# Attention and two expert layers on one core: the instruction order laid out by another scheduling model

## The chip, the cores and the metric

The kernel runs on one core of a Trainium2 chip. The metric is the device time of one launch in microseconds (us); lower is better. A core has several engines that run side by side, each with its own list of instructions that it works through in order: PE (TensorE: matrix products, with PEld for its weight loads), DVE (VectorE) and ACT (ScalarE) for elementwise work, POOL (GpSimd) for elementwise work as well, and SP (SyncE), which here issues nearly all transfers (DMAs). An instruction that needs the result of another engine waits at the head of its list, and everything behind it on that engine waits with it.

## The reference

Three layers follow each other. For 4 batches and 8 heads of 576 positions with 64 features, the attention is the sum of two parts; then come two layers on the 2304 x 512 result:

```python
out_d = sm_attn(q_d, k_d, v_d)            # q, k, v averaged over groups of 4 positions
out_up = np.repeat(out_d, factor, axis=2)
mask = np.abs(pos[:, None] - pos[None, :]) < factor
...                                       # softmax over the masked band of 7 positions
out_local = np.matmul(attn, v)
return (out_up + out_local).astype(np.float32)
...
a = x @ w1
b = x @ w2
h = a * b @ w3
return (h @ w_out).astype(np.float32)     # d_ff 1024
...
h = x @ w_in
g = h * (1.0 / (1.0 + np.exp(-h)))
return (g @ w_out).astype(np.float32)     # d_ff 2048
```

The weights arrive as 64-bit floating-point numbers.

## The kernel before

**Weights.** A 64-bit weight is loaded as two 32-bit words (tile `st`, the load is issued on SP). A piece of 128 x 512 weights is turned into 32-bit numbers by one ACT instruction (the absolute value of the high word) and four DVE instructions: L162 (limits), L166 (shift), L171 (sign) and L176 (low bits). Where a weight is needed as the sum of a high and a low part, ACT copies the high part and DVE subtracts (L191). These pieces are called `dec`, `w_wo`, `w_w` while they are decoded and `w_wA`, `w_wB`, `w_wC`, `w_wx`, `w_wy` when they are ready. A product of two such split numbers takes three matrix passes.

**Opening (to about 150 us).** Two things run side by side. `wprime` (L456) multiplies the two last matrices of the first layer pair into one: 128 matmuls `wp`, whose results DVE and ACT move out as `w_wC` (L470). And the attention runs in 16 units (two heads of one batch each). A unit has these steps: DVE adds groups of four positions (`qkd`, L237); PE makes the scores `sd` of the averaged attention (L284) and `s` of the banded one (L333); DVE and ACT form the softmax (maxima `md` L291 and `ml` L343, the masked copy `band` L340, of which there is one buffer); PE transposes (`td` L301, `tl` L352); PE sums `od` (L318) and `ol` (L376); DVE copies `od` to `ods` (L323), adds both (`xf`, L390), and splits the sum (`x`, L401). The sums `ol` of a unit are 36 small matmuls in two halves, `ol_0` (20) and `ol_1` (16). The halves read different partitions, which is different rows of PE's array: the first from partition 0 on, the second from 64 on. They are issued by turns:

```python
for h in range(2):
    ...
        k = slice(64 * h, 64 * h + KW)
        ...
        nc.tensor.matmul(
            op[h][r, c0:c0 + QW], lhsT=v[k, sub, c, r], rhs=ET[k, c, q0:q0 + QW],
            start=True, stop=True,
        )
```

**Middle (150 to about 495 us).** The `ab` groups (L548) multiply `x` by the two first matrices; DVE multiplies the two results (`cf`, L562); the `y` groups (L581) follow and go to memory. The remaining attention units stand between these groups.

**End (495 us on).** `h` groups (L719, 12 matmuls each) and `o` groups (L746, 9 each) for 6 tiles of 384 tokens, 16 of each per tile. Between an `h` group and its `o` group stand ACT's sigmoid `sg` (L725), DVE's product `gf` (L727) and its rounding copy `g` (L729), and POOL's low part of `g` (L730). In program order an `o` group comes three `h` groups after its own. During the first of the six tiles DVE still decodes the 32 weight pieces of the last layer, between these products. The last copies go out through six DMAs (L759).

**What sets the order.** The kernel is written as one sequence of operations with buffers of limited number (`bufs=`). The framework takes this sequence and lays out the order of each engine's instructions itself; it puts in the waits that the data and the buffers need. Which of two independent instructions of one engine comes first is the framework's choice. The choice is made inside the context that `kernel` opens at L830. No line of the functions named above sets it.

## Time and profile before

| | us |
|---|---|
| time, median of 3 runs (lowest, highest) | 911.85 (910.41, 914.21) |
| the profiled execution, its own time | 913.42 |
| its span in the trace | 911.6 |
| PE busy | 879.0 |
| DVE busy | 420.1 |
| ACT busy | 293.6 |
| POOL busy | 256.8 |

The span runs from the first to the last recorded event. "Busy" is the time in which an engine works on an instruction. The mean granted clock of PE over the span was 0.983 of full speed (2.4 GHz); it falls to half (1.2 GHz) in some stretches. In rows of a timeline, consecutive instructions of one kind are drawn together, the first number is the start in us, the second how long the group took, and a bracket at the end tells how long the engine sat idle ahead of it and whose result it waited for.

### The profile page before, as it was taken

To read this page: it belongs to the slowest core of one execution; us is meant where nothing else is said; L and a number is where in the kernel's file an instruction comes from. 1 tells how busy PE (TensorE), PEld (TensorE's weight loads), DVE (VectorE), ACT (ScalarE), POOL (GpSimd) and SP (SyncE) were. 2 spreads that over 40 slices of the span, in tenths; PEclk is the share of its full clock that TensorE was granted. 3 is DMA by queue.
4 is the path that set the end of the run, shared out by engine and by line. 5 is a ranking of instruction groups with operands and counts; after the bars stand their busy time and mean duration, and the time that the engine had idled before them with its cause. 6 is when DMAs were issued, how large, how long until landed. Compare 5 with 4: busy or idle time off the path is not lost.

```text
span 911.6 us, 17876 instructions
## 1 busy us (share of the span) xinstructions
PE 879.0 (96%) x7248; PEld 779.5 (86%) x7248; DVE 420.1 (46%) x894; ACT 293.6 (32%) x935; POOL 256.8 (28%) x262
## 2 busy tenths in 40 slices
PE   5899999999999999999999989999999999999997
PEld 3454688999999999999999878999898999989896
DVE  5989996342423333138459994222222222222221
ACT  5565754443233333332244432111111111111111
POOL 2000324342333334232211535224223224222221
PEclk9799999999899999999999999999999999999999
DMA  8667641323222221116035451201100100100101
GB/s 308 196 220 233 213 134 47 99 75 104 78 73 73 64 76 33 47 57 193 14 99 173 133 164 56 53 1 33 38 1 1 36 1 1 35 1 0 35 1 35
DMA packets 27282, 73.68 MB, mean 81 GB/s; under 512 B 3264, under 2 KB 10432, under 8 KB 27200
## 3 DMA queue, kind: packets, MB, share of 16 engines
q1 hardware_dynamic: 27200, 72.55, 25.9%
q8 instruction: 57, 0.93, 0.4%
q14 instruction: 25, 0.20, 0.1%
HBM read 63.09 MB, written 9.44 MB: 80 GB/s over the span
## 4 chain that ended last, share of the span: by engine, by line
PE 78%; DVE 11%; DMA 4%; issue 3%; ACT 2%; POOL 1%; SPq 0%; DVEq 0%; ACTq 0%; POOLq 0%
PE o L746 20%; PE h L719 19%; PE ab L548 17%; PE y L581 9%; PE wp L456 5%; DMA st<-wb 3%; PE ol L376 3%; DVE dec L171 2%; DVE dec L176 2%; PE tl L352 1%; DVE dec L162 1%; PE sd L284 1%; PE td L301 1%; PE s L333 1%; DVE dec L166 1%
## 5 line engine op out<-in xcount | busy, mean ns | idle before, releaser
L730 POOL TENSOR_TENSOR g<-gf,g 128x384 fp32r<-128x384 f32 x96 | 105.0, 1093 | 273.9 <-DVE g L729 258.9
L727 DVE TENSOR_TENSOR gf<-h,sg 128x384 f32<-128x384 f32 x96 | 53.4, 557 | 256.1 <-ACT sg L725 256.1
L725 ACT ACTIVATE sg<-h 128x384 f32<-128x384 f32 x96 | 47.0, 490 | 289.1 <-PE h L719 289.1
L548 PE MATMUL ab<-x,w_wB 128*128 128x320 f32 (+1 forms) x768 | 115.3, 304 | 1.9 <-DVE x L401 0.5
L548 PEld LDWEIGHTS ab<-x,w_wB 128*128 128x128 f32 x768 | 106.7, 192 | 3.7 <-DVE x L401 0.8
L581 PE MATMUL y<-c,w_wC 128*128 128x320 f32 (+1 forms) x768 | 108.9, 298 | 0.0
L548 PE MATMUL ab<-x,w_wA 128*128 128x320 f32 (+1 forms) x768 | 108.9, 300 | 0.0
L548 PEld LDWEIGHTS ab<-x,w_wA 128*128 128x128 f32 x768 | 104.2, 190 | 0.5
L581 PEld LDWEIGHTS y<-c,w_wC 128*128 128x128 f32 x768 | 103.1, 188 | 0.6 <-DVE cf L562 0.3
L566 POOL TENSOR_TENSOR c<-cf,c 128x320 fp32r<-128x320 f32 (+1 forms) x64 | 54.9, 858 | 153.1 <-DVE c L565 135.1
L562 DVE TENSOR_TENSOR cf<-ab,af 128x320 f32<-128x320 f32 (+1 forms) x64 | 29.0, 453 | 113.7 <-PE ab L548 108.8
L456 PE MATMUL wp<-w_wo,w_w 128*128 128x512 f32 x128 | 63.4, 641 | 6.9 <-DVE w_w L176 6.8
L746 PE MATMUL o<-w_wA,g 128*128 128x512 f32 x216 | 55.3, 399 | 4.7 <-POOL g L730 3.6
L719 PE MATMUL h<-yhl,w_wC 128*128 128x384 f32 x288 | 55.2, 341 | 0.0
L719 PE MATMUL h<-yhl,w_wB 128*128 128x384 f32 x288 | 54.1, 337 | 0.4 <-ACT yo L590 0.4
L719 PE MATMUL h<-yhl,w_wA 128*128 128x384 f32 x288 | 54.2, 337 | 0.0
L746 PE MATMUL o<-w_wB,g 128*128 128x512 f32 x216 | 54.1, 394 | 0.0
L719 PEld LDWEIGHTS h<-yhl,w_wC 128*128 128x128 f32 x288 | 52.1, 192 | 2.3
L746 PE MATMUL o<-w_wC,g 128*128 128x512 f32 x216 | 54.0, 395 | 0.0
L456 PEld LDWEIGHTS wp<-w_wo,w_w 128*128 128x128 f32 x128 | 24.7, 204 | 33.8 <-issue 24.5
L719 PEld LDWEIGHTS h<-yhl,w_wB 128*128 128x128 f32 x288 | 50.8, 188 | 2.6 <-ACT yo L590 0.7
L719 PEld LDWEIGHTS h<-yhl,w_wA 128*128 128x128 f32 x288 | 51.0, 188 | 2.2
(101 smaller groups left out, 1277.8 us busy)
## 6 DMA issues: line engine op xcount, KB each, us to landing
st<-wb SPq DMA_DIRECT2D x32, 512.0 KB
qk<-qk SPq DMA_DIRECT2D x16, 579.0 KB
st<-w3t SPq DMA_DIRECT2D x16, 512.0 KB
st<-w SPq DMA_DIRECT2D x16, 512.0 KB
vr<-vr SPq DMA_DIRECT2D x16, 320.0 KB
st<-ydram SPq DMA_DIRECT2D x12, 384.0 KB
out<-os SPq DMA_DIRECT2D x36, 128.0 KB
st<-wo SPq DMA_DIRECT2D x8, 512.0 KB
```

What stands on the lines that cost most here:

```text
L171: nc.vector.scalar_tensor_tensor(out=v, in0=st[:, :, 1], scalar=-0x40000000, in1=v, op0=ALU.bitwise_and, op1=ALU.bitwise_or,)
L376: nc.tensor.matmul(op[h][r, c0:c0 + QW], lhsT=v[k, sub, c, r], rhs=ET[k, c, q0:q0 + QW], start=True, stop=True,)
L456: nc.tensor.matmul(acc, lhsT=w3v[:, k, j * P:(j + 1) * P], rhs=wov[:, k, :], start=(gp == 0 and k == 0), stop=(gp == 3 and k == 1),)
L548: nc.tensor.matmul(acc[:, :N], lhsT=wv[:, i, w, kk, :], rhs=x[:, j, :], start=(n == 0), stop=(n == 11),)
L562: nc.vector.tensor_tensor(out=cf, in0=acc[:, :N], in1=C.pop("af"), op=ALU.mult)
L566: nc.gpsimd.tensor_tensor(out=c[:, 1], in0=cf, in1=c[:, 0].bitcast(F32), op=ALU.subtract)
L581: nc.tensor.matmul(acc[:, :N], lhsT=WP[kf // 2][:, i, kf % 2, ec * P:(ec + 1) * P], rhs=c[:, j, :], start=(kf == 0 and n == 0), stop=(kf = ...
L719: nc.tensor.matmul(acc[:, :TT], lhsT=w[:, i, kk, :], rhs=y[:, j, kk, :], start=(n == 0), stop=(n == 11),)
L725: nc.scalar.activation(sg, acc[:, :TT], AF.Sigmoid)
L727: nc.vector.tensor_tensor(out=gf, in0=acc[:, :TT], in1=sg, op=ALU.mult)
L730: nc.gpsimd.tensor_tensor(out=g[:, 1], in0=gf, in1=g[:, 0].bitcast(F32), op=ALU.subtract)
L746: nc.tensor.matmul(acc_ps[t][j], lhsT=g[:, a, j * P:(j + 1) * P], rhs=w[:, b, 512:1024], start=(f == 0 and n == 0), stop=(f == 15 and n == 2),
```

## The change

The source of the operations stays as it is. One argument of the context in which they are laid out is added. With it the framework chooses the order of each engine's instructions by its own timeline model (an estimate of when each instruction would start and end) where it used its default order before.

```diff
-    with tile.TileContext(nc) as tc:
+    with tile.TileContext(nc, schedule_with_timeline_sim=True) as tc:
         tile_model(tc, *args)
```

What the change does is therefore seen in the order alone. Three places are shown, each before and after. In the rows a name such as `x_0_1261` is a tile with its number, the word ahead of it is the operation, and a number behind an x tells how many stand in a row.

The first is DVE near 115 us in the trace of before, where the split `x_0_1261` of the fourth unit is made. Before:

```order
L470 TENSOR_TENSOR w_wC<-wp_2_821,w_wC 128x512
L470 TENSOR_TENSOR w_wC<-wp_3_823,w_wC 128x512
L323 COPY ods_1219<-od_1214 128x144
L162 TENSOR_SCALAR dec<-dec 128x512
L390 TENSOR_TENSOR xf_0_1259<-ol_0_1221,ods_1219 128x320
L166 TENSOR_SCALAR dec<-dec 128x512
L390 TENSOR_TENSOR xf_1_1264<-ol_1_1222,ods_1219 128x256
L171 SCALAR_TENSOR_TENSOR dec<-st,dec 128x512
L162 TENSOR_SCALAR dec<-dec 128x512
L176 SCALAR_TENSOR_TENSOR dec<-st,dec 128x512
L263 TENSOR_SCALAR sm<-sm 128x9
L401 TENSOR_TENSOR x_0_1261<-xf_0_1259,x_0_1261 128x320
```

And after, on the same engine:

```order
L253 TENSOR_SCALAR sm<-md_1540 128x3
L191 TENSOR_TENSOR w_wB<-dec,w_wB 128x512
L162 TENSOR_SCALAR dec<-dec 128x512
L401 TENSOR_TENSOR x_0_1261<-xf_0_1259,x_0_1261 128x320
L176 SCALAR_TENSOR_TENSOR dec<-st,dec 128x512
L166 TENSOR_SCALAR dec<-dec 128x512
L171 SCALAR_TENSOR_TENSOR dec<-st,dec 128x512
L263 TENSOR_SCALAR sm<-sm 128x9
L176 SCALAR_TENSOR_TENSOR dec<-st,dec 128x512
L266 RECIPROCAL sm<-sm 128x9
L470 TENSOR_TENSOR w_wC<-wp_0_785,w_wC 128x512
```

The four L470 copies (two of them are seen above, the first of them below) stood ahead of `x_0_1261` and now stand behind it, and a softmax step of the next unit (`md_1540`) stands ahead of it.

The second is PE in the middle, at one of the attention units between `ab` groups. Before:

```order
L318 MATMUL od_3280<-EdT_3060,vd_3085 64x144 x4
L376 MATMUL ol_0_3287<-ET_3073,vw_2991 64x32 x11
L376 MATMUL ol_1_3288<-ET_3073,vw_2991 64x32 x10
L376 MATMUL ol_0_3287<-ET_3073,vw_2991 64x32
L376 MATMUL ol_1_3288<-ET_3073,vw_2991 64x32 x2
L376 MATMUL ol_0_3287<-ET_3073,vw_2991 64x32 x2
L376 MATMUL ol_1_3288<-ET_3073,vw_2991 64x32 x2
```

And after, at the same unit:

```order
L318 MATMUL od_3280<-EdT_3060,vd_3085 64x144 x4
L376 MATMUL ol_0_3287<-ET_3073,vw_2991 64x32 x19
L376 MATMUL ol_1_3288<-ET_3073,vw_2991 64x32 x16
L376 MATMUL ol_0_3287<-ET_3073,vw_2991 64x32
L548 MATMUL ab_0_7_1_3338<-x_0_1718,w_wA 128x320 x3
```

Before, the halves go on by turns of two to the unit's end; now they stand one behind the other. The same holds at units 5, 6, 7 and 9 to 14; at unit 8 the halves stood apart before as well, and at unit 15 they take turns in both orders. Of the early units, unit 1 had its halves apart and now has them by turns.

The third is DVE in the first tile of the end stage, at the eighth product `g_7`. Before:

```order
L171 SCALAR_TENSOR_TENSOR dec<-st,dec 128x512
L727 TENSOR_TENSOR gf_7_6662<-h_7_6647,sg_7_6660 128x384
L191 TENSOR_TENSOR w_wC<-dec,w_wC 128x512
L729 CAST g_7_6664<-gf_7_6662 128x384
L176 SCALAR_TENSOR_TENSOR dec<-st,dec 128x512
L162 TENSOR_SCALAR dec<-dec 128x512
```

And after:

```order
L191 TENSOR_TENSOR w_wC<-dec,w_wC 128x512
L176 SCALAR_TENSOR_TENSOR dec<-st,dec 128x512
L727 TENSOR_TENSOR gf_7_6662<-h_7_6647,sg_7_6660 128x384
L171 SCALAR_TENSOR_TENSOR dec<-st,dec 128x512
L162 TENSOR_SCALAR dec<-dec 128x512
L729 CAST g_7_6664<-gf_7_6662 128x384
L191 TENSOR_TENSOR w_wC<-dec,w_wC 128x512
```

One decoding step stood between `gf_7` and `g_7`, and now two do; at `g_0` to `g_5` it was one and now it is four. Counted from the start of the program, the whole list ahead of `g_7` is shorter than before by one L166, one L171, one L176 and two L191, and the list ahead of `g_9` by one each of L162, L171, L176 and L191.

## Rows read from the trace of the kernel before

**Rows 1.** Part 1 of the page: busy time of each engine.

```profile
PE 879.0 (96%) x7248; PEld 779.5 (86%) x7248; DVE 420.1 (46%) x894; ACT 293.6 (32%) x935; POOL 256.8 (28%) x262
```

**Rows 2.** PE's waits: engine, line, releaser, us in total, times, longest.

```profile
PE sd L284 <- DVE qkd L237: 7.3, 1, 7.3
PE wp L456 <- DVE w_w L176: 6.8, 2, 4.3
PE o L746 <- POOL g L730: 4.5, 3, 2.7
PE td L301 <- DVE xf L390: 2.7, 1, 2.7
```

**Rows 3.** Windows: stretch, length, busy PE, PEld, DVE, ACT, POOL; clock, DMA, GB/s.

```profile
30.00:40.00 10.00, 7.73 (x39) 4.09 (x40) 10.00 (x28) 7.18 (x30) 0.00 (x0) 0.55 0.72 239
...
60.00:80.00 20.00, 17.25 (x148) 8.66 (x147) 19.87 (x45) 13.79 (x51) 0.00 (x0) 1.00 0.70 237
...
120.00:140.00 20.00, 19.67 (x241) 18.52 (x240) 20.00 (x45) 11.84 (x38) 6.48 (x6) 1.00 0.35 110
...
160.00:410.00 250.00, 249.42 (x3164) 236.79 (x3163) 87.35 (x213) 92.60 (x394) 86.18 (x101) 0.99 0.23 70
```

**Rows 4.** Timeline of DVE in the opening: start, us, instruction, idle before.

```profile
5.89 1.35 DVE L237 TENSOR_REDUCE qkd<-qk 128x288 f32<-128x1152 f32 x1 [5.89 <-DMA qk<-qk]
...
8.68 0.42 DVE L162 TENSOR_SCALAR w_w<-w_w 128x512 f32<-128x512 f32 x1
9.02 0.68 DVE L176 SCALAR_TENSOR_TENSOR w_wo<-st,w_wo 128x512 int32<-128x512 int32 x1
9.62 0.60 DVE L291 TENSOR_REDUCE md<-sd 128x3 f32<-128x432 f32 x1
...
23.39 0.61 DVE L291 TENSOR_REDUCE md<-sd 128x3 f32<-128x432 f32 x1 [4.32 <-PE sd L284]
...
108.22 0.68 DVE L470 TENSOR_TENSOR w_wC<-wp,w_wC 128x512 fp32r<-128x512 f32 x1
...
115.48 0.47 DVE L401 TENSOR_TENSOR x<-xf,x 128x320 fp32r<-128x320 f32 x1
```

**Rows 5.** Timeline of PE: the first `ab`; `ol`, halves apart and by turns.

```profile
108.11 3.20 PE L548 MATMUL ab<-x,w_wB 128*128 128x320 f32 x20
111.25 1.12 PE L376 MATMUL ol<-ET,vw 38*64 38x32 f32 x32
...
163.07 1.65 PE L376 MATMUL ol<-ET,vw 38*64 38x32 f32 x72
...
226.85 1.35 PE L376 MATMUL ol<-ET,vw 38*64 38x32 f32 x40
```

**Rows 6.** Windows, shorter stretches: columns as in rows 3.

```profile
95.40:100.60 5.20, 5.20 (x132) 3.83 (x130) 5.20 (x13) 3.74 (x12) 0.91 (x1) 1.00 0.54 129
...
226.00:229.00 3.00, 2.99 (x67) 2.33 (x66) 2.73 (x6) 0.24 (x1) 2.14 (x3) 1.00 0.15 49
229.00:233.00 4.00, 4.00 (x35) 3.94 (x32) 2.21 (x4) 0.86 (x2) 2.48 (x4) 0.50 0.64 168
233.00:237.00 4.00, 4.00 (x20) 4.00 (x19) 0.53 (x2) 0.42 (x1) 0.91 (x1) 0.64 0.42 137
...
535.00:552.00 17.00, 12.59 (x54) 10.60 (x55) 16.97 (x31) 6.96 (x13) 7.47 (x4) 0.94 0.53 166
```

**Rows 7.** Timelines of PE and POOL near the end of the first tile.

```profile
537.26 2.12 PE L746 MATMUL o<-w_wA,g 128*128 128x512 f32 x8 [0.95 <-POOL g L730]
...
545.00 3.52 POOL L730 TENSOR_TENSOR g<-gf,g 128x384 fp32r<-128x384 f32 x1 [3.64 <-DVE g L729]
...
548.58 2.70 PE L746 MATMUL o<-w_wA,g 128*128 128x512 f32 x8 [2.65 <-POOL g L730]
```

**Rows 8.** Timelines of PE and of SP's queue, the last of the span.

```profile
901.46 4.27 PE L746 MATMUL o<-w_wy,g 128*128 128x512 f32 x18
...
905.01 3.67 SPq L759 DMA_DIRECT2D out<-os  x6
```

## The prediction

> **What bounds the kernel now.** I read the page's busy times first. PE is busy for 879.0 of 911.6 us, the next engine, DVE, for less than half of that [rows 1]. So the time is PE's own work plus the few places where PE waits or runs slowly, and a new order can act in three ways: on PE's waits, on how long the same matmuls take, and on PE's clock.
>
> Next, PE's waits by releaser [rows 2]. Apart from 7.3 us for the first data, all the large ones name DVE, or POOL behind DVE: 6.8 for a decoded weight, 4.5 for `g`, 2.7 in the attention. Then the windows say where DVE is the narrow engine [rows 3]. In 60 to 80 and 120 to 140 us DVE is busy for 19.87 and 20.00 of 20 us while PE still has gaps: this is the opening, where DVE's list sets the pace. In 160 to 410 us it is the other way: PE is busy for 249.42 of 250 us and DVE for 87.35. There no wait can be gained, and only the duration of the matmuls counts. In 535 to 552 us DVE is busy for 16.97 of 17 us again and PE for 12.59 [rows 6].
>
> **The opening.** What DVE does ahead of a product decides when PE gets it. I counted DVE's instructions ahead of `x_0_1261` in both orders. After, eight fewer of about 0.60 us stand there (two L176, one L171, one L191, four L470), one L162 and one L166 fewer, and one L390 fewer; two L237, one L291 and one L253 more. The step lengths are read from the starts of neighbouring rows: L176 at 9.02 is followed at 9.62 (0.60), L162 at 8.68 at 9.02 (0.34); an L470 has the same busy 0.68 as the L176, so I give it and the L191 the same 0.60; an L237 is busy for 1.35 and an L291 for 0.60, less the same overlap of some 0.07 with the next [rows 4]. For L390 I take 0.4 and for L253 0.1, as estimates after the 0.47 of the similar L401. That is 8 x 0.60 + 2 x 0.34 + 0.4 = 5.9 saved against 2 x 1.28 + 0.53 + 0.1 = 3.2 added: 2.7 us earlier. Then the holes in DVE's list. It waits 5.89 us for the first data and 4.32 us for unit 1's scores [rows 4]. After, one L162 and one L166 stand ahead of the first L237 and go into the first hole: 0.7 us. Unit 1's `qkd` moves up from the 29th to the 22nd place on DVE, and PE makes its scores earlier, so part of the 4.32 is filled. Bounds: nothing and 4.3. I take 1.1, since the order puts 3 more decodes ahead of the place and PE is itself busy there. Together -4.5 us. Below, the whole could come to nothing, because PE has to wait for the decoded `w_w` later anyway (its longest wait, 4.3 us [rows 2]); above, -9 with the hole filled (2.7 + 0.7 + 4.3) and some of the slow clock of 30 to 40 us (0.55 [rows 3]) gone.
>
> **The middle.** Here the same work takes another length. A unit's 72 matmul records take 1.65 us when the halves go by turns; apart they take 1.35 for the first half and 1.12 for the second, 2.47 together [rows 5]. So apart costs 0.82. When the second half follows the first at once, as the changed order has it, the start and end of a run are paid once and not twice, so I take 0.65, with 0.5 and 0.82 as the ends. It holds for units 5, 6, 7 and 9 to 14, nine units: +5.9 us (4.5 to 7.4), all of it on the path, since PE has no idle time there. Unit 1's gain of the same size lies in the opening, where DVE binds, and I count it at nothing.
>
> On this term the Trainium skill speaks with two tongues. Its page "TensorE: Matmul & The Clock Gate" (Part 2, step by step) says that PE pulls a weight load ahead of running matmuls when the row groups differ or when it goes to the background buffer. By the second half of that rule an order without turns would hide its loads too, the term would be 0 and the sum 5.9 us lower. Its Part 3 says that the loads overlap only when the row groups differ; the rows above, 1.65 against 2.47, agree with this one.
>
> **The end stage.** PE waits twice there, at 537.26 (and just ahead of it, for the same `g_7`) and 2.65 us at 548.58 for `g_9`, whose POOL step at 545.00 took 3.52 us [rows 7]. DVE is full there. Ahead of `g_7` the changed list is shorter by four steps of 0.60 and one of 0.34, that is 2.7 us; ahead of `g_9` by three and one, 2.1 us. So `g_7` comes soon enough and `g_9` 2.1 us sooner. Against this, three more decodes stand between `gf` and `g` early in the stage, and the weights come later by what `g` gains. I take -2.5, with +1 and -5 (both waits and the slow clock behind the second one gone) as the ends.
>
> **The tail.** The last `o` matmuls run one and then two per result instead of three and three, so the first result is finished two matmuls later: 4.27 us for 18 [rows 8] gives 0.24 each, +0.5. The six DMAs of 3.67 us begin after it. I take +0.4.
>
> **The sum.** From the profiled 913.42: -4.5 + 5.9 - 2.5 + 0.4 = 912.7. The profiled execution lies 1.6 above the median of 911.85, so the time is 911.1; I say 911.
>
> **Rivals.** First, the waits go as far as they can. The opening gives 9 and the end stage 5: 913.42 - 9 + 5.9 - 5 + 0.4 - 1.6 = 904. For it: DVE has gaps of 10 us in the first 24 us while it sets the pace afterwards. Against it: the work behind these gaps depends on PE and on transfers, too.
>
> Second, slower: the clock. At unit 8, where `ol` stood apart, the clock was 1.00 in 226 to 229 us, 0.50 in 229 to 233 and 0.64 in 233 to 237, without any idle time of PE [rows 6]. 4 x 0.50 + 4 x 0.36 = 3.4 us were lost. After, nine more units have such an unbroken stretch of small matmuls. If three of them are followed by such a fall, the time is 911.1 + 10.2 = 921; from two on the kernel is slower by over 0.5%. Against it: 5.2 us of small matmuls at 95.40 kept 1.00 [rows 6]. The same page of the Trainium skill, "Why this matters for your kernels", asks only for no long idle gaps of PE between bursts; by that rule this rival has no ground and the sum stays, while unit 8's fall without a gap speaks against the rule.
>
> Third, nothing comes of the opening: PE's new order has unit 4's scores `s` ahead of the last `wp` matmuls, and the one `band` buffer can hold it there until unit 3 is transposed. Then the term is 0 and the time 915.6.
>
> **How the numbers follow.** A measurement of this kernel can tell about 0.5%, 4.6 us, from no change: faster is below 907.3, slower above 916.4. Forecast 0.30 (its own range 907 to 916), first rival 0.30, second 0.24, third 0.16. Faster takes most of the first and a fifth of the forecast, 0.34. The same takes most of the forecast, over half of the third and the near ends of the others, 0.36. Slower is the second rival and what of the third lies above, 0.30. The range of 8 in 10 goes from 902.5 to 922.
>
> **What would show it.** Right: the 72 records of a unit between 200 and 400 us take about 2.2 us each; `ab` begins near 104 to 106 us instead of 108.11 [rows 5]; PE's wait ahead of `g_9` is under 1 us. Wrong: a unit's records still at 1.65 (the middle term is false); the clock under 0.9 in more than two windows between 160 and 410 us (the second rival); the wait for `w_w` as long as before and a new one ahead of the first `ab` (the third).

## The result and the profile after

The changed kernel takes 918.12 us (median of 9 runs, 914.44 to 922.17) and the kernel before 911.85 (9 runs beside them, 910.41 to 915.30). The ratio is 1.0064 with a 95% interval of 1.0040 to 1.0088: slower by 6.3 us, where 911 was forecast. The profiled execution of after took 919.92 us with a span of 918.1, 6.5 more than the span of before.

Part 1 of the page of after, against [rows 1]: PE works 7.2 us longer on the same 7248 matmul records.

```profile
PE 886.2 (97%) x7248; PEld 787.0 (86%) x7248; DVE 425.9 (46%) x894; ACT 293.9 (32%) x935; POOL 250.0 (27%) x262
```

PE's waits in after, with the columns of [rows 2]: engine, line, releaser, us in total, times, longest.

```profile
PE sd L284 <- DVE qkd L237: 7.8, 1, 7.8
PE tl L352 <- ACT ET L356: 5.3, 3, 2.4
PE sd L284 <- ACT Ed L257: 3.5, 2, 2.5
PE wp L456 <- DVE w_w L176: 3.4, 2, 1.9
PE ab L548 <- DVE w_wA L191: 2.1, 1, 2.1
PE o L746 <- POOL g L730: 1.6, 2, 1.1
```

The wait for decoded weights is halved (6.8 to 3.4) and the wait for `g` falls from 4.5 to 1.6. But two releasers are new: the transposes `tl` and the scores `sd` wait 8.8 us for ACT. The timeline of PE shows where these stand (start, us, instruction, idle before):

```profile
27.11 0.95 PE L284 MATMUL sd<-qkd 64*64 64x144 f32 x12 [2.48 <-ACT Ed L257]
...
54.83 0.29 PE L352 MATMUL tl<-ident,band 128*38 128x128 f32 x1 [2.35 <-ACT ET L356]
...
81.04 0.71 PE L284 MATMUL sd<-qkd 64*64 64x144 f32 x8 [1.02 <-ACT Ed L257]
...
109.38 0.29 PE L352 MATMUL tl<-ident,band 128*38 128x128 f32 x1 [2.28 <-ACT ET L356]
...
122.71 3.77 PE L548 MATMUL ab<-x,w_wB 128*128 128x320 f32 x24
...
154.65 2.55 PE L548 MATMUL ab<-x,w_wA 128*128 128x320 f32 x11 [2.09 <-DVE w_wA L191]
...
173.66 2.08 PE L376 MATMUL ol<-ET,vw 38*64 38x32 f32 x72
```

The first `ab` begins at 122.71 instead of 108.11 [rows 5], and a unit's 72 `ol` records take 2.08 us instead of 1.65. The windows of after that answer to [rows 3] and [rows 6] (stretch, length, busy PE, PEld, DVE, ACT, POOL; clock, DMA, GB/s):

```profile
30.00:40.00 10.00, 10.00 (x81) 5.77 (x80) 9.70 (x23) 5.77 (x27) 0.00 (x0) 0.52 0.52 169
...
60.00:80.00 20.00, 19.04 (x199) 9.70 (x198) 17.47 (x38) 13.29 (x46) 0.00 (x0) 0.91 0.51 164
...
60.00:120.00 60.00, 53.79 (x560) 28.82 (x560) 53.62 (x115) 36.35 (x132) 3.72 (x3) 0.91 0.60 192
...
160.00:410.00 250.00, 249.83 (x3133) 239.95 (x3132) 88.15 (x212) 90.34 (x395) 80.49 (x96) 0.97 0.23 69
535.00:552.00 17.00, 16.47 (x83) 14.58 (x82) 16.40 (x28) 6.58 (x13) 6.66 (x5) 1.00 0.45 148
```

In 60 to 80 us DVE has 2.5 us of idle time where it had 0.13. Over 60 to 120 us neither DVE nor PE is full (each is idle for some 6 us) and the clock is 0.91. In the middle the clock goes from 0.99 to 0.97. In the end stage PE is busy for 16.47 of the 17 us in which it was busy for 12.59.

Where the time went: the n-th `ab` matmul is a mark that both orders pass with the same work done. At the 250th (the last of the opening; the same number of matmul records ahead of it, up to one) after lies 12.8 us behind; at the last `ab` 13.6 behind; from the first `h` (13.2 behind) to the last `h` it gains 7.2 and is 6.0 behind. So the opening costs 12.8 us, the middle 0.4 (to the first `h`), the end stage gives back 7.2 and the tail costs 0.5. The opening, up to the 250th `ab`, in one window of before and one of after (the two ends are set to a tenth of a us and lie 12.7 apart):

```profile
0.00:179.20 179.20, 159.70 (x1704) 113.10 (x1705) 141.64 (x313) 101.79 (x368) 35.50 (x45) 0.95 0.56 181
```

```profile
0.00:191.90 191.90, 168.14 (x1703) 116.97 (x1704) 145.49 (x313) 102.01 (x368) 31.76 (x45) 0.93 0.52 169
```

Length less PE's busy time is PE's waiting: 19.5 and 23.8 us. Of its busy time PE spends 15.8 us at half clock before and 26.7 after, and each us at half clock costs half a us. So 4.3 of the 12.7 are waits, 5.4 are the clock, and 3.0 are left over. This is the account of one execution of each.

### The profile page after: what moved, and what is told of

Its sections match the earlier page's. It is cut to its first block, busy times and chain, and to the rows that moved or that the text cites. A ratio compares the mean times of both kernels' runs of the same rounds, so it can differ in the third digit from the quotient of the medians.

```text
span 918.1 us, 17871 instructions
## 1 busy us (share of the span) xinstructions
PE 886.2 (97%) x7248; PEld 787.0 (86%) x7248; DVE 425.9 (46%) x894; ACT 293.9 (32%) x935; POOL 250.0 (27%) x262
## 4 chain that ended last, share of the span: by engine, by line
PE 73%; DVE 11%; DMA 8%; ACT 4%; issue 3%; POOL 0%; SPq 0%; DVEq 0%; ACTq 0%; POOLq 0%
PE o L746 20%; PE h L719 19%; PE ab L548 18%; PE y L581 10%; DMA st<-w3t 3%; PE ol L376 2%; ACT band L257 2%; DMA st<-wb 2%; DMA st<-w 2%; DVE dec L171 1%; DMA st<-wo 1%; DVE dec L176 1%; PE sd L284 1%; DVE dec L162 1%; DVE w_wA L191 1%
## 5 line engine op out<-in xcount | busy, mean ns | idle before, releaser
L730 POOL TENSOR_TENSOR g<-gf,g 128x384 fp32r<-128x384 f32 x96 | 101.0, 1053 | 270.3 <-DVE g L729 255.8
L548 PE MATMUL ab<-x,w_wA 128*128 128x320 f32 (+1 forms) x768 | 111.2, 302 | 2.1 <-DVE w_wA L191 2.1
L548 PE MATMUL ab<-x,w_wB 128*128 128x320 f32 (+1 forms) x768 | 112.5, 303 | 0.0
L566 POOL TENSOR_TENSOR c<-cf,c 128x320 fp32r<-128x320 f32 (+1 forms) x64 | 57.1, 893 | 154.9 <-DVE c L565 143.2
L456 PE MATMUL wp<-w_wo,w_w 128*128 128x512 f32 x128 | 66.6, 665 | 3.4 <-DVE w_w L176 3.4
```

The costliest lines, as they stand in the source:

```text
L456: nc.tensor.matmul(acc, lhsT=w3v[:, k, j * P:(j + 1) * P], rhs=wov[:, k, :], start=(gp == 0 and k == 0), stop=(gp == 3 and k == 1),)
L548: nc.tensor.matmul(acc[:, :N], lhsT=wv[:, i, w, kk, :], rhs=x[:, j, :], start=(n == 0), stop=(n == 11),)
L566: nc.gpsimd.tensor_tensor(out=c[:, 1], in0=cf, in1=c[:, 0].bitcast(F32), op=ALU.subtract)
L730: nc.gpsimd.tensor_tensor(out=g[:, 1], in0=gf, in1=g[:, 0].bitcast(F32), op=ALU.subtract)
```

## The experiments

All are compared with the kernel before on the same chip; a ratio stands with its 95% interval.

**Is it the order alone, and which part of it?** The numbers of each engine's instructions in the wanted order stand in a table, and the default model lays the kernel out with edges that only fix this order:

```diff
     with tile.TileContext(nc) as tc:
         tile_model(tc, *args)
+        hold_order(tc)
...
+def hold_order(tc):
+    traced = {i.name: i for i in tc.nc.cur_bb.bb.instructions}
+    info = mybir.DependencyInfo(mybir.DependencyClass.NoSync, mybir.DependencyReason.DATA)
+    for text in ORDERS.values():
+        ...
+        for one, two in zip(row, row[1:]):
+            tc.add_manual_dep(two, one.name, info, reason="order")
```

hold_after has the table of after. In open_before the first 813 instructions of PE, 290 of DVE, 247 of ACT, 41 of POOL and 64 of SP stand as before. In ol_turns the halves of `ol` go by turns in units 5, 6, 7 and 9 to 14, as in this piece of PE's list. best has both.

```diff
-L376 MATMUL ol_0_1986<-ET_1797,vw_1726 64x32 x19
-L376 MATMUL ol_1_1987<-ET_1797,vw_1726 64x32 x16
+L376 MATMUL ol_0_1986<-ET_1797,vw_1726 64x32 x11
+L376 MATMUL ol_1_1987<-ET_1797,vw_1726 64x32 x10
 L376 MATMUL ol_0_1986<-ET_1797,vw_1726 64x32
+L376 MATMUL ol_1_1987<-ET_1797,vw_1726 64x32 x2
```

By turns means here that 11 matmuls of the first half stand ahead, then 10 of the second, and only the last 15 of the 36 take turns. A matmul of `ol` leaves two records in the trace.

> The framework's default model, but a table holds each engine's instructions in exactly the changed kernel's order (edges of order alone, no waits). If the order is all that the change does: 1.006 of the kernel before, about 918 us. Rival, that something else of the timeline model (which buffer a tile gets, which waits are set) costs the time: 1.00, about 912 us.

> The table holds the order of before up to the end of the opening (the first 250 ab matmuls on PE and what belongs to them on the other engines) and the changed order from there on. Theory A, the loss is made in the opening (the traces differ by 12.8 us there) and the end stage gives 7 back: 918 - 12.8, about 905 us, 0.993. Rival B, the loss is made by the small matmuls that stand apart in the middle and the clock that falls after them: the opening gives nothing, 917 to 918 us, 1.006.

> The changed order, but in the nine units 5 to 7 and 9 to 14 the 36 small ol matmuls take turns again as before; nothing else moves. From the traces a unit takes 1.86 us apart and 1.43 by turns: 9 x 0.43 = 3.9 us less, 914 us, if only their own length counts (theory A). Rival B, the clock falls too (three falls of 3.4 us at half clock after unit 7 and units 9 to 14): 5 us more than that, about 909 us.

> Both: the opening in the order of before, the ol turns as before, all else in the changed order, so the end stage above all. Theory A: 905 - 3.9 = about 901 us, 0.988 of before. If the end stage's 7 us hung on the opening being late: 908 to 912 us.

| run | us | ratio |
|---|---|---|
| hold_after | 916.45 | 1.0073 [1.0045, 1.0101] |
| open_before | 907.23 | 0.9956 [0.9937, 0.9974] |
| ol_turns | 910.91 | 0.9999 [0.9982, 1.0016] |
| best | 901.56 | 0.9891 [0.9873, 0.9909] |

The order alone makes the change. The opening is worth 9.2 us, the halves 5.5, and the two add up: 916.45 - 9.2 - 5.5 = 901.7, against 901.56. What is left of after in best (the end stage and the rest of the middle) is 9.1 us faster than before.

end_only is the order of before with the end stage of after; ol_apart is before with the halves apart in the nine units.

> The order of before up to the end stage, the changed order in the end stage (all engines). From the traces the end stage gains 7.1 to 7.5 us: 904 to 905 us, 0.992. Rival: the gain hangs on what the changed order does ahead of it (decodes done earlier because PE is late): 908 to 912 us.

> The order of before, but in units 5 to 7 and 9 to 14 the ol halves stand apart as in the changed order; nothing else moves. Length alone, 9 x 0.43 = 3.9 us: 915.5 us, 1.004. With the clock falling behind three more units (3.4 us at half clock each, 1.7 lost): 5 us more, 920 us, 1.009 to 1.010.

end_only took 904.63, ratio 0.9942 [0.9919, 0.9964], that is 5.7 us less; ol_apart 917.33, ratio 1.0079 [1.0055, 1.0103], 7.0 more. In its trace a unit's `ol` takes 2.08 us:

```profile
163.13 2.08 PE L376 MATMUL ol<-ET,vw 38*64 38x32 f32 x72
183.46 2.08 PE L376 MATMUL ol<-ET,vw 38*64 38x32 f32 x72
```

9 x 0.43 = 3.9 of the 5.5 to 7.0 are the length itself. The clock is the rest. Behind the opening (195 to 500 us) the thirteen profiles with the halves apart, those below among them, have 3.4 to 13.7 us at half clock, 9.6 in the mean; the seven by turns have 0 to 6.8, 2.9 in the mean. The difference of 6.7 us is worth 3.3. The profile of ol_apart has only 6.8, as that of before has, so these two profiles don't show it, but the runs do. Every run has a mean granted clock, and its span times what this clock lacks to 1.00 is what half clock cost it, at most (PE may be idle in part of it). That is 15.6 us for ol_apart (6 runs) and 11.5 for before (11 runs beside them), which is 4.1 of the 7.3 us between their means; 17.4 for hold_after (7 runs) and 13.8 for ol_turns (12 runs), which is 3.6 of 6.5. Each of the two differences has an interval of about 3 us either way.

Of the 9.1 us by which best beats before, 5.7 are the end stage; some 3.4 come from the rest of the middle's order and were not taken apart. From the 250th `ab` to the first `h`, PE's busy time less half of that at half clock is 310.9 us in the profile of before and 307.5 in that of best, so it is PE's own work that gets shorter there.

**What in the opening?** The chain of waits of after names the round trip of a weight piece (load, L152, the four steps on DVE, the next load into the buffer so freed), where that of before names PE's own `wp`. From L162 to the end of L176 a piece takes 6.0 us in after and 4.0 before, in the mean of the 40 pieces of the opening, since other instructions stand between its steps. Four ways to shorten this were tried on the order of after: compact has the four steps of a piece together on DVE (at the place of the first), act_sink moves 15 of ACT's L152 behind the instructions that feed PE, urgent puts what after newly has ahead of a `w_w` piece behind it again, and st3b has a fifth staging buffer. best_compact does to best what compact does to after. A piece of DVE's list in compact and one in urgent, against hold_after, and the edit of st3b:

```diff
 L162 TENSOR_SCALAR w_w_224<-w_w_224 128x512
 L166 TENSOR_SCALAR w_w_224<-w_w_224 128x512
+L171 SCALAR_TENSOR_TENSOR w_w_224<-st,w_w_224 128x512
+L176 SCALAR_TENSOR_TENSOR w_w_224<-st,w_w_224 128x512
 L291 TENSOR_REDUCE md_146<-sd_138 128x3
```

```diff
-L291 TENSOR_REDUCE md_580<-sd_572 128x3
-L266 RECIPROCAL sm<-sm 128x3
-L237 TENSOR_REDUCE qkd_819<-qk_399 128x288
 L176 SCALAR_TENSOR_TENSOR w_w_266<-st,w_w_266 128x512
```

```diff
-            st = home.tile([P, 512, 2], I32, tag="st", name="st", bufs=2)
+            st = home.tile([P, 512, 2], I32, tag="st", name="st", bufs=3 if home is stg2 else 2)
```

> The changed order, but in the opening DVE's four decoding steps of a weight piece (L162, L166, L171, L176) stand one behind the other at the place of the first; the other engines keep the changed order. Theory T1: the changed order spreads the four steps (6.52 us from the first to the end of the last, 3.77 before), and as SP issues the load that reuses a staging buffer 0.07 us after the last step, the loop of four buffers sets the opening's pace (14.3 us a round against 12.4). Contiguous they take 1.9 us, a round falls to 10 to 12: the opening gives back most of its 9 to 13 us, 904 to 909 us. Theory T2, ACT's L152 stand ahead of what PE waits for (8.8 us of PE's waits name ACT): no gain, 915 to 918 us.

> The changed order, but on ACT in the opening 15 of the L152 that stand directly ahead of transposed copies and exponentials (L305, L308, L356, L257, L269) stand behind up to nine of them. T2: PE's waits on ACT (5.9 + 2.9 us in the held order's trace) shrink by half or more, 909 to 913 us. T1: the loop of staging buffers is as long as before or a little longer, 915 to 918 us.

> The changed order throughout, with three staging buffers instead of two in the second staging pool of the opening (five in all instead of four). T1: a round of the loop serves five pieces, so loads are issued earlier; L152 waits less for loads (41.7 us of ACT's waits), 907 to 912 us. Rival T3, the places of PE's own instructions (unit 1's and unit 4's scores ahead of the products) cost the time: 915 to 918 us. T2 expects the small part of T1.

> The order of best (opening and ol turns as before, end stage changed), with the four decoding steps of a piece contiguous on DVE in the opening. T1: the opening of before is paced by the same loop, 12.4 us a round, and gets shorter by some us too: 894 to 899 us. If DVE's own work is the pace there: as best, 901 to 902 us.

> The changed order on PE, ACT, POOL and SP; on DVE, in the opening, what the changed order newly put ahead of a decoded w_w piece (maxima and pooled queries of later units, decoding of w12 pieces, 7.5 us in sum ahead of the last piece, 10.0 ahead of the last but two) stands behind it again, so that the work ahead of each w_w piece is the same as before within 0.8 us (3 us at one). Theory T4: the opening is late because DVE does less urgent work first, and PE's products need w_w: 906 to 910 us. Rival T5: the opening's order on the other engines costs as much by itself (PE's units earlier, ACT's list), then DVE's order is no remedy and the deferred softmax steps hold PE: 915 us or more.

| run | us | ratio |
|---|---|---|
| compact | 935.18 | 1.0263 [1.0234, 1.0292] |
| act_sink | 925.64 | 1.0157 [1.0127, 1.0187] |
| st3b | 914.94 | 1.0047 [1.0020, 1.0073] |
| best_compact | 921.01 | 1.0115 [1.0087, 1.0143] |
| urgent | 940.37 | 1.0340 [1.0313, 1.0367] |

Three of the remedies cost 9 to 24 us, where one theory or the other had each of them gain; best_compact is 19.5 us behind best, and the fifth buffer's gain of some 1.5 us isn't told from nothing. PE's waits in urgent show why moving decoding up doesn't help:

```profile
PE sd L284 <- DVE qkd L237: 21.2, 3, 10.4
...
PE wp L456 <- DVE w_w L176: 1.3, 1, 1.3
```

The wait for `w_w` is nearly gone, and the attention waits 21.2 us for `qkd` (7.8 of them for the first data, as in after), which now stands behind the decoding. These runs speak against the remedies, but not yet on whether decoding is the cause. Two pairs do. In thin_open_before and thin_after the four steps work on 64 of 512 columns; in aside_open_before and aside_after they stand at their places but on a small tile of their own, so that nothing waits for them. Both pairs have the orders of open_before and hold_after, and the steps of the last layer are left whole. The weights ahead of it are then not the decoded ones.

```diff
-                    out=v, in0=v, scalar1=3, scalar2=0x3FFFFFF8,
+                    out=v[:, :ncol], in0=v[:, :ncol], scalar1=3, scalar2=0x3FFFFFF8,
```

```diff
+            if pair[0][0][0] != "wb":
+                steps_aside(len(todo))
+                return
```

> The order of before in the opening and of after behind it, with the four decoding steps L162, L166, L171 and L176 working on 64 of the 512 columns of each weight piece until the last layer (so its weights are not the decoded ones; the number and the order of all instructions are kept). It is the base for thin_after, which differs from it in the order of the opening alone. With full decoding steps this pair was hold_after 916.45 and open_before 907.23, 9.2 us apart. Theory (what after's opening pays for is DVE's decoding, which stands later in DVE's list there): with steps of some 0.1 us the base gets faster by some 5 to 10 us, 897 to 902, and thin_after by 9 us more than that. Rival (the loss is PE's own order, the clock or transfers): the base gets faster by the same amount as thin_after.

> The order of after throughout, with the same four decoding steps on 64 of 512 columns until the last layer (weights not decoded there; number and order of instructions kept). Theory, DVE's decoding is what the order of after pays for: the two are then within 3 us of each other, 897 to 904, and the first ab is within 4 us of that of thin_open_before (12.8 apart between after and before). Rival, PE's own order, the clock or the transfers: this kernel stays 8 us or more behind thin_open_before, and the first ab 10 us or more. In between: both have a share, in proportion.

> As thin_open_before (opening in the order of before, the rest in that of after), but until the last layer the four decoding steps L162, L166, L171 and L176 stand at their places in DVE's list and work on a small tile of their own, 32 columns wide: neither the products nor the raw-weight buffers wait for them any longer, only for ACT's L152 (the weights are not the decoded ones). Base for aside_after. thin_open_before took 894.7 us; both theories let this one take 885 to 894.

> As thin_after (the order of after throughout), with the same four steps aside, so that no product and no load waits for their places in DVE's list. With steps cut short but still waited for, the two orders of the opening were 12.4 us apart. Theory (what costs in after's opening is where the decoding steps stand: behind attention steps on DVE that wait for PE and ACT, so L162 to L176 took 5.4 us of waiting in thin_after against 1.7): the distance to aside_open_before falls to 4 us or less, and the first ab to within 5 us. Rival (PE's own order, ACT's places or the clock): the distance stays at 8 us or more.

| run | us | ratio |
|---|---|---|
| thin_open_before | 894.67 | 0.9834 [0.9810, 0.9858] |
| thin_after | 907.05 | 0.9963 [0.9945, 0.9982] |
| aside_open_before | 895.24 | 0.9817 [0.9789, 0.9844] |
| aside_after | 904.21 | 0.9902 [0.9866, 0.9939] |

The distance is 12.4 us with short steps and 9.0 with steps that nobody waits for, against 9.2 with whole steps. So the two orders stay about as far apart when decoding is out of the way: most of what after's opening pays for is something else, and the theory of the round trip falls. The windows to the 250th `ab` show what remains when decoding is out of the way, first aside_open_before, then aside_after:

```profile
0.00:167.60 167.60, 155.48 (x1703) 110.39 (x1704) 84.09 (x313) 100.33 (x368) 28.99 (x45) 0.98 0.58 194
```

```profile
0.00:177.50 177.50, 163.04 (x1704) 113.78 (x1705) 87.61 (x313) 100.65 (x368) 29.68 (x45) 0.94 0.55 183
```

DVE is busy for half of the time in both. PE waits 12.1 and 14.5 us, and its busy time grows by 7.6 us with the same matmuls: the part at half clock goes from 4.8 to 19.8 us, which is worth 7.5. The waits differ by 2.4 us here and by 5.6 between open_before and hold_after, so some 3 us of waiting do go with the decoding. The windows of these two, open_before first:

```profile
0.00:178.20 178.20, 159.61 (x1703) 113.74 (x1704) 141.09 (x313) 101.90 (x368) 34.96 (x45) 0.96 0.55 182
```

```profile
0.00:190.80 190.80, 166.61 (x1704) 115.94 (x1705) 146.51 (x313) 102.06 (x368) 31.46 (x45) 0.93 0.52 170
```

The same account for all orders of the opening (one profile each; "half clock" is the part of PE's busy time that runs at half clock, and the last column is busy less half of it, fillers taken off):

| order of the opening | to 250th `ab` | PE busy | waits | half clock | PE's own work |
|---|---|---|---|---|---|
| before | 179.2 | 159.7 | 19.5 | 15.8 | 151.8 |
| after | 191.9 | 168.1 | 23.8 | 26.7 | 154.8 |
| open_before | 178.2 | 159.6 | 18.6 | 11.2 | 154.0 |
| hold_after | 190.8 | 166.6 | 24.2 | 26.6 | 153.3 |
| thin_open_before | 168.0 | 155.4 | 12.6 | 3.4 | 153.7 |
| thin_after | 183.1 | 164.3 | 18.8 | 19.6 | 154.5 |
| aside_open_before | 167.6 | 155.5 | 12.1 | 4.8 | 153.1 |
| aside_after | 177.5 | 163.0 | 14.5 | 19.8 | 153.1 |
| act_sink | 200.4 | 171.9 | 28.5 | 38.0 | 152.9 |
| compact | 205.0 | 173.0 | 32.0 | 38.8 | 153.6 |
| urgent | 210.5 | 172.7 | 37.8 | 39.0 | 153.2 |
| fill_after (below) | 188.3 | 170.9 | 17.4 | 10.2 | 155.6 |

PE's own work is 152 to 156 us in every order. The length of the opening is this, the waits, and half of the time at half clock. Between open_before and hold_after the waits are 5.6 us of the 12.6 and the clock 7.7. The other profiles that have one of these openings whole agree: 12.4 to 15.8 us at half clock with that of before (best, end_only, ol_apart), 22.6 and 23.3 with that of after (st3b, ol_turns).

The clock's share is less sure than these profiles make it look. Behind the opening, where both have the same order, the profile of open_before has 13.7 us at half clock and that of hold_after 6.8; this gives 3.4 us back, so that the spans of the two profiles differ by 9.0 us and not by 12.6. Over all runs the clock cost hold_after 17.4 us and open_before 14.7: 2.7 of the 9.7 us between their means, with 3.1 either way, and 7.0 are waits and PE's work. In the two pairs without decoding its share is larger: 6.2 of 12.2 us (thin) and 5.6 of 8.3 (aside), with 3 to 4 us either way.

**Does the half clock come from the waits?** fill_after puts 42 matmuls that add zero to a running sum into PE's waits in the order of after; best_fill puts 16 into the one long wait of best (4.3 us ahead of `wp`).

```diff
+    def filler(kind, acc):
+        for _ in range(FILL.get((kind, n_mm[kind]), 0)):
+            nc.tensor.matmul(acc[:, :P], lhsT=zero, rhs=ident, start=False, stop=False)
+        n_mm[kind] += 1
```

> The order of after throughout (hold_after, 916.45), with 42 matmuls of 128x128 that add zero to a running sum, placed on PE where it stood idle in the opening: 8 at 24.2 us, 10 at 51.7, 2 at 79.5, 5 at 95.5, 9 at 105.7 and 8 at 151.4, some 0.2 us each and a little shorter together than the wait they stand in. The result is unchanged. Theory (most of the opening's loss is PE at half clock, and the falls follow PE's waits of 0.6 to 2.8 us): the falls at 55, 83, 110 and 154 us go (1.7 us each) and perhaps the one of 10.2 us at 28 gets shorter: 908 to 912, and time at half clock up to the 250th ab falls from 26.6 us to under 16. Rival (the falls have another cause, such as the kind of matmuls that run): the falls stay, and the time is 916 or, by fillers that overrun the waits, up to 919.

> The version best (901.56: opening as before, ol by turns, the rest as after) with 16 such matmuls in the one long wait of its opening (4.3 us at 28.9 us, ahead of wp for its decoded weight). The result is unchanged. Theory: the fall of 10.2 us behind that wait goes or gets shorter, up to 5 us less: 896 to 900. Rival (the fall has another cause): 901 to 903.

The timeline of PE in fill_after near 106 us; its lines are shifted, L75 is the filler (two records each, so x18 is nine of them), L361 is `tl`:

```profile
106.31 2.17 PE L75 MATMUL wp<-ident,zero 128*128 128x128 f32 x18
108.70 0.29 PE L361 MATMUL tl<-ident,band 128*38 128x128 f32 x1 [0.22 <-ACT ET L365]
```

The windows around this place, hold_after first (the wait, then the fall), then fill_after:

```profile
103.00:110.10 7.10, 4.62 (x54) 2.74 (x53) 5.92 (x13) 3.76 (x9) 0.74 (x1) 1.00 0.38 149
110.10:113.50 3.40, 3.40 (x71) 2.22 (x68) 3.40 (x8) 0.62 (x1) 0.01 (x1) 0.51 0.50 135
```

```profile
80.00:120.00 40.00, 39.78 (x440) 23.23 (x439) 37.14 (x78) 23.43 (x91) 4.17 (x3) 1.00 0.65 214
```

With the waits filled, the clock stays at 1.00 through the 40 us in which hold_after had two falls, and the falls at 28, 55 and 154 us are gone too; one of 3.4 us at 35 and one of 6.8 at 65.7 are there instead. Each of these two stands behind a wait that was left (0.96 and 0.70 us from 28.40 on, 1.53 us at 64.09). Half clock in the opening goes from 26.6 to 10.2 us, and over all runs the clock costs 13.1 us (11 runs) where it cost hold_after 17.4: the falls do follow the waits. Not all of them do: the fall at 174.9 us, with no wait close ahead of it, is gone in this profile too. The same in best (its wait and the stretch behind), then in best_fill:

```profile
28.00:33.20 5.20, 0.90 (x14) 0.63 (x13) 5.20 (x12) 1.40 (x3) 0.00 (x0) 0.88 0.50 168
32.00:42.20 10.20, 9.00 (x40) 4.47 (x41) 10.20 (x28) 8.45 (x36) 0.00 (x0) 0.50 0.78 256
```

```profile
28.00:33.20 5.20, 4.78 (x50) 4.38 (x46) 5.20 (x12) 1.28 (x4) 0.00 (x0) 1.00 0.51 178
32.00:42.20 10.20, 9.41 (x59) 4.93 (x59) 10.20 (x29) 8.35 (x35) 0.00 (x0) 1.00 0.75 259
```

The long fall of 10.2 us is gone. Yet neither kernel is faster: fill_after took 917.22 us, ratio 1.0059 [1.0039, 1.0078], and best_fill 903.13, ratio 0.9908 [0.9877, 0.9938]. The forecasts of 908 to 912 and 896 to 900 missed. The fillers take PE time themselves (10.2 us in fill_after, against 6.8 us of waits and 8.2 us of clock that they save; PE's own work is 2.3 us longer as well, which stays open: at the 250th `ab` 2.5 us were won, and the whole run shows nothing of it). In best_fill DVE is busy throughout both windows, as in best, and PE meets a new wait of 1.4 us at 42.9.

**The fastest version.** best with the fifth buffer of st3b:

> The order of best with five staging buffers in the opening instead of four. T1 (the loop of staging buffers paces the opening in any order): 895 to 899 us. If DVE's own work and its order pace it: as best, 900 to 902 us.

It took 900.33 us, ratio 0.9883 [0.9862, 0.9905], and is the fastest found; from best, 0.9891, it isn't told apart.

## Why the prediction was wrong

**What bounds the kernel** held: PE's work, its waits and its clock are the three things that moved.

**The opening, -4.5 forecast, +9.2 by exchange (+12.8 in the two profiles).** This step failed, and in its first sentence: "What DVE does ahead of a product decides when PE gets it." Two things were wrong with it. First, the product: `x_0_1261` was counted 4.5 us earlier and came 2.4 us later, 117.87 against 115.48 [rows 4], and it was not what PE needed in either order. In before the first `ab` begins at 108.11 [rows 5], 7.4 us ahead of this `x`, and the `ab` that did wait for it lost 0.51 us:

```profile
116.01 1.44 PE L548 MATMUL ab<-x,w_wB 128*128 128x320 f32 x8 [0.51 <-DVE x L401]
```

PE's new list has the last `wp` and the rest of an `ol` ahead of the first `ab`, which began 4.4 us after `x` was ready. DVE in after:

```profile
117.87 0.49 DVE L401 TENSOR_TENSOR x<-xf,x 128x320 fp32r<-128x320 f32 x1
```

Secondly, the resource: with DVE's decoding taken out, the two orders are about as far apart as with it. What the new order did to PE's list was not counted at all, and the sum had no term for the clock. The new list has `sd` and the last `tl` of some units at points where ACT is not done with the exponentials and copies that they wait for (8.8 us of new waits for ACT), and it spreads the waiting: before has four waits of 0.7 us and more after the first data, 10.8 us together; after has nine, 15.3 us together. Several of these are followed by half clock. In the two profiles this costs 5.4 us more than in before, and the waits 4.3 more. The third rival ("nothing comes of the opening") named a hold-up of PE's list behind the attention, and was the nearest in kind; it priced it at no loss.

Which single placement makes the waits stays open: no run has the whole list of one engine from one order and the others' from the other. act_sink moves ACT's L152 alone; in its first 205 us PE's waits for ACT fall from the 9.1 us of hold_after to 7.3, and those for DVE rise from 14.8 to 21.0.

**The middle, +5.9 forecast, +5.5 to +7.0 by exchange.** The mechanism was right, halves apart cost on the path. The size per unit was off: 0.43 us, not 0.65, since 72 records in one piece take 2.08, less than the 1.35 and 1.12 of two pieces [rows 5] by 0.39. Most of the gain of the turns lies in the last 15 matmuls of a unit: their records take 0.44 us in before at 163 us and 0.76 in after at 173. The second rival has a share as well, and its sign came: in the profile of after four falls of 3.4 us lie between 160 and 410 us (13.6 us at half clock, against 6.8 before), net 3.4 us lost, a third of that rival's 10.2; the first of the four, at 176.1, stands ahead of the 250th `ab` and is in the opening's account above. By the runs the clock is 3.6 to 4.1 us of what the halves cost. In the two profiles the middle as a whole shows only 0.4, because the rest of its order saves PE some 3 us of work.

The Trainium skill's page "TensorE: Matmul & The Clock Gate" ("Why this matters for your kernels") asks for no long idle gaps. Its Part 1 ("A second HAM failure mode: psum-queue depth-cycling") also tells of a kernel where frequent micro-idles made the clock go up and down. By the first, none of after's waits of 0.5 to 2.5 us would matter; the falls at 83.9 and 111.2 us, behind waits of 1.02 and 2.28 us, speak for the second. The fall at 176.1 us, behind no wait, fits neither.

**The end stage, -2.5 forecast, -5.7 by exchange (-7.2 in the profiles).** Right in sign, too small. PE's waits for `g` fall by 2.9 us and none over 1.1 us is left, against 2.65 at 548.58 [rows 7]:

```profile
550.50 2.13 PE L746 MATMUL o<-w_wA,g 128*128 128x512 f32 x8 [0.53 <-POOL g L730]
556.05 2.13 PE L746 MATMUL o<-w_wA,g 128*128 128x512 f32 x8 [1.09 <-POOL g L730]
```

In 500 to 560 us end_only keeps PE busy for 59.06 us; before had 54.24 there with a clock of 0.97. Before, then end_only:

```profile
500.00:560.00 60.00, 54.24 (x261) 47.76 (x260) 52.77 (x92) 22.53 (x41) 26.07 (x16) 0.97 0.42 133
```

```profile
500.00:560.00 60.00, 59.06 (x296) 52.85 (x295) 52.68 (x90) 23.15 (x41) 28.53 (x21) 1.00 0.40 126
```

The forecast counted the steps ahead of two products; the gain is nearly all of PE's waits of the stage (6.1 to 1.6 us), the fall at 549.9 us (1.7 us) and a little more. That is beyond the far end of the range, -5.

**The tail, +0.4 forecast.** From the last `o` group to the DMAs it was 3.55 us [rows 8] and is 4.02, +0.5:

```profile
907.47 4.27 PE L746 MATMUL o<-w_wy,g 128*128 128x512 f32 x18
```

```profile
911.49 3.67 SPq L759 DMA_DIRECT2D out<-os  x6
```

**The sum.** By exchange: +9.2 + 5.5 - 5.7 - 3.4 (rest of the middle) = +5.6, against +5.8 of hold_after and +6.3 of after. Had the opening been counted at +9.2 instead of -4.5, the forecast would have been 924.7: the other terms erred by 6.6 us the other way, most of it the end stage and the middle's rest. That the forecast of 911 lies only 7 us off is in part luck, then.

The clock, which the sum left to a rival, is the larger part of the result. Over all runs it cost hold_after 17.4 us and before (20 runs beside it) 11.6: 5.8 of the 6.2 us between their means, with 2.8 either way. In waits and PE's work the stages about cancel.

## What to carry to other kernels

When an order changes, read PE's own list first and ask at each small matmul which engine has to be done there; counting what stands ahead of a product on another engine says nothing as long as PE's list asks for something else first. Price each wait of the matrix engine twice, for itself and for the slow clock that may follow. Compare the clock over many runs and not in one profile alone. Whether one long wait is cheaper than many short ones isn't shown here. An order that a model lays out is not one decision: exchange it stage by stage, and keep the stages that win (here 901.6 us, where the whole of either order takes 910.6 or more).

## What the runs showed of the hardware

- Many waits of PE of 0.6 to 2.8 us are followed by stretches at half clock. Filling them with matmuls on zeros took the falls away (26.6 to 10.2 us at half clock in one opening; 0.50 to 1.00 in 32 to 42 us of the other). Not every such wait is followed by a fall: behind 2.67 us at 67.3 in before the clock stayed at 1.00.
- A fall without any wait came again, in after at 176.1 us, behind a stretch of small matmuls in which PE was busy throughout:

```profile
172.00:176.10 4.10, 4.10 (x91) 3.67 (x90) 0.99 (x4) 1.55 (x9) 1.46 (x2) 1.00 0.15 51
176.10:179.50 3.40, 3.40 (x14) 3.40 (x14) 0.52 (x2) 0.76 (x2) 0.58 (x1) 0.50 0.69 196
```

- Two halves of small matmuls on different rows of the array take 2.08 us one behind the other and 1.65 when the last 15 of the 36 take turns, 72 records each: 29 against 23 ns a record. In these last 15 it is 0.76 against 0.44 us.
- The clock also makes runs of one kernel differ: of the nine runs of after the fastest took 914.44 us at a mean granted clock of 0.986 and the slowest 922.17 at 0.969.
